# Retention followed by a gated feed-forward block: the row transposes of chunks 2 to 5 are issued by ScalarE instead of SyncE

## The chip, the cores and the metric

The kernel runs on one core of a Trainium2 chip. A core has five engines with an instruction queue each: TensorE (PE, matrix products), VectorE (DVE), ScalarE (ACT, activation functions and copies), GpSimd (POOL) and SyncE (SP, which here only issues DMAs). Every engine executes its own queue in order, and the queues meet only at semaphores. The metric is the device time of one execution in microseconds, lower is better.

## The reference

Two stages are joined. The first is a recurrence over 768 positions for 4 batches and 8 heads of 64 elements, with a decay per head:

```python
gamma = 1.0 - 2.0 ** (-5.0 - np.arange(H))
for t in range(S):
    state = gamma * state + einsum('bhd,bhe->bhde', k[:, :, t], v[:, :, t])
    y[:, :, t] = (1/sqrt(D)) * einsum('bhd,bhde->bhe', q[:, :, t], state)
```

Its 3072 rows of 512 (heads side by side) go through a feed-forward block:

```python
rms = sqrt(mean(x * x, axis=-1) + 1e-6)
xn = x / rms * rms_g
g = xn @ w_gate                      # 512 x 1536
out = (g * sigmoid(g) * (xn @ w_val)) @ w_out
```

Inputs and output are float32.

## The kernel before

The 768 positions are cut into 6 chunks of 128 positions. A piece of work belongs to a chunk c (0 to 5) and a batch b (0 to 3). Inside a chunk the recurrence is a masked product of q and k times v; between chunks a state per batch is carried. Matrix operands are bfloat16, sums are float32 in PSUM, which is used as eight banks.

The order of all work is written out by hand in the string ORDER (lines 17 to 100). Each word is one step: a letter for the function, then its arguments, after "@" the engine (D, A, P, S for DVE, ACT, POOL, SP) and after "/" the PSUM banks. Each engine executes its own steps in the order of the string; semaphores between engines, and between DMA queues, follow from the data and from buffer reuse. The steps that matter here, for one c and b:

- Lq, Lk, Lv load float32 rows (line 314, for these chunks on SP); Cq, Ck and V convert or scale them (V on ACT is eight calls, one a head, line 356). tq and tk transpose q and k by DMA on SP (line 387).
- A multiplies kT and qT into two banks for each batch it names (A.3.2/0546: batches 2 and 3 of chunk 3, banks 0 and 5, 4 and 6; line 403). M0 and M1 mask the result on DVE (line 426). Y multiplies it by v and adds the state's part (lines 441 and 445).
- S is ACT's sum of squares of y (xsq, line 458, or 455 where y lies in two banks). R makes 1/rms on POOL (lines 468, 470). N writes the normalised rows xn, 128 x 512, on DVE (line 482, or 479).
- The feed-forward block needs xn transposed, as xnT. In chunks 0 and 1 PE transposes it (X, line 495) and XE copies it out of PSUM. In chunks 2 to 5 there is no X: XE is a DMA transpose of xn into xnT, issued by SP (line 501).
- g and v multiply xnT by the two weights (line 549), 128 columns a step for all 512 rows of a chunk, so the first of them needs the XE of all four batches. s is Silu on ACT (line 559), which empties the bank of g; h multiplies by v's bank into hT on DVE (line 567).
- d multiplies hT by the output weights (line 574), o copies the result to o_sb on ACT or DVE (line 146, a helper), st stores it (line 587, SP). B and U carry the state (lines 541 and 534).

So the XE steps stand in SP's queue between loads, stores and the transposes of q and k. In the order string the 16 XE words of chunks 2 to 5 are XE.2.0, XE.2.1, XE.2.3, XE.2.2; XE.3.1 and, further down, XE.3.0, XE.3.2, XE.3.3; XE.4.0, XE.4.1, XE.4.3, XE.4.2; XE.5.0, XE.5.3, XE.5.2, XE.5.1.

xn has a ring of 4 buffers and xnT one of 2. DMA completions of SP are counted on eight semaphores in turn, so each DMA also waits until the one eight before it has landed.

Of the kernel before, what the change touches and what calls it, by code (L numbers as in the profile page):

```python
# [49 lines left out]
s.1.4.5.0.4 K.1.3/4 v.1.4.5.0.4/0 S.2.0 U.1.3@D v.1.5.6.0.4/1 Cq.3.1@P h.1.9.10.0.4 R.2.0 h.1.4.5.0.4 A.2.2/5264  # L50
h.1.5.6.0.4 N.2.0 Y.2.1/7 Lk.3.1@S M0.2.3 M0.2.2 V.2.3@P B.1.3 S.2.1 d.1.1.0.10/1 K.2.0/3 tq.3.0 Ck.3.1@A
d.1.1.10.12 M1.2.3 R.2.1 M1.2.2 tk.3.0 Lv.2.2@S Y.2.3/6 S.2.3 V.2.2@P d.1.0.0.10/0 K.2.1/2 Y.2.2/5 tq.3.1
Lk.3.2@S S.2.2 N.2.1 R.2.3 d.1.2.0.12/7 R.2.2 U.2.1@D o.1.1@A XE.2.0@S Lk.3.3@S tk.3.1 K.2.3/4 N.2.3 U.2.0@D
N.2.2 Lq.3.3@S XE.2.1@S d.1.3.0.12/3 U.2.3@D A.3.0/2641 M1.3.1 d.1.0.10.12 XE.2.3@S XE.2.2@S M0.3.1 st.0.3@S
M0.3.0 st.0.2@S st.0.0@S B.2.1 Lv.3.1@S g.2.5.6.0.4/5 Lv.3.0@S o.1.3@A g.2.0.1.0.4/1 v.2.8.9.0.4/4 s.2.5.6.0.4
v.2.5.6.0.4/2 s.2.0.1.0.4 M1.3.0 Lq.3.2@S Lq.4.1@S Ck.3.3@D g.2.10.11.0.4/6 g.2.1.2.0.4/1 h.2.5.6.0.4 o.1.0@A
v.2.10.11.0.4/0 g.2.8.9.0.4/2 B.2.0 Cq.3.3@P s.2.10.11.0.4 Lk.4.0@S s.2.8.9.0.4 o.1.2@A g.2.6.7.0.4/5
# [1 line left out]
g.2.11.12.0.4/3 V.3.1@A Cq.4.1@P s.2.6.7.0.4 Lv.3.2@S h.2.10.11.0.4 s.2.3.4.0.4 tk.3.3 Lq.4.0@S h.2.8.9.0.4  # L59
Lv.3.3@S K.3.1/2 s.2.1.2.0.4 h.2.3.4.0.4 tk.3.2 g.2.4.5.0.4/5 B.2.3 h.2.6.7.0.4 U.3.1@D V.3.2@D tq.3.2 Lq.5.0@S  # L60
st.1.0@S v.2.11.12.0.4/4 K.2.2/7 U.2.2@D s.2.11.12.0.4 Y.3.1/6 tq.4.1 st.1.2@S S.3.1 h.2.11.12.0.4 v.2.1.2.0.4/1
h.2.1.2.0.4 R.3.1 g.2.7.8.0.4/2 st.1.3@S v.2.7.8.0.4/4 Ck.4.1@P s.2.7.8.0.4 N.3.1 XE.3.1@S g.2.2.3.0.4/3
h.2.7.8.0.4 Ck.4.0@D s.2.4.5.0.4 st.1.1@S A.3.2/0546 M1.3.2 s.2.2.3.0.4 v.2.2.3.0.4/7 g.2.9.10.0.4/3 V.3.0@D
M0.3.2 V.3.3@A s.2.9.10.0.4 v.2.4.5.0.4/5 M1.3.3 h.2.2.3.0.4 Lk.5.2@S Y.3.0/2 Lv.4.0@S M0.3.3 v.2.9.10.0.4/6
Y.3.3/3 Lv.4.1@S B.2.2 K.3.3/7 S.3.0 h.2.4.5.0.4 S.3.3 R.3.0 K.3.0/5 h.2.9.10.0.4 Y.3.2/0 Lv.4.2@S Cq.4.0@P
d.2.2.0.12/1 R.3.3 K.3.2/4 N.3.0 S.3.2 N.3.3 d.2.1.0.10/2 d.2.1.10.12 XE.3.0@S Lq.5.2@S R.3.2 N.3.2 Ck.5.2@D
XE.3.2@S d.2.3.0.12/3 U.3.3@D XE.3.3@S U.3.2@D Lk.4.2@S o.2.2@D Lq.4.2@S Lv.5.3@S U.3.0@D d.2.0.0.10/4 tk.4.0
g.3.6.7.0.4/5 tk.4.1 o.2.3@A o.2.1@D g.3.0.1.0.4/0 v.3.6.7.0.4/7 s.3.6.7.0.4 tq.4.0 v.3.0.1.0.4/1 s.3.0.1.0.4
g.3.10.11.0.4/6 V.4.2@D B.3.1 Lv.4.3@S Lk.4.3@S Cq.5.0@P g.3.5.6.0.4/5 s.3.10.11.0.4 h.3.0.1.0.4 g.3.9.10.0.4/3
d.2.0.10.12 v.3.5.6.0.4/0 h.3.6.7.0.4 Lq.4.3@S s.3.5.6.0.4 v.3.9.10.0.4/1 v.3.10.11.0.4/2 h.3.5.6.0.4  # L70
# [6 lines left out]
M1.4.3 v.3.7.8.0.4/4 tq.5.2 M0.4.2 st.2.3@S M0.4.3 S.4.0 s.3.11.12.0.4 Y.4.1/0 h.3.7.8.0.4 M1.4.2 Cq.5.3@P R.4.0  # L77
v.3.11.12.0.4/7 h.3.11.12.0.4 K.4.1/4 Lv.5.1@S Y.4.2.2 S.4.1 Y.4.3.2 S.4.2 V.5.1@P d.3.1.0.10/6 tk.5.3 tk.5.2
N.4.0 R.4.1 tk.5.1 st.2.0@S d.3.1.10.12 S.4.3 tq.5.3 N.4.1 R.4.3 o.3.1@A R.4.2 d.3.0.0.10/1 B.4.3 N.4.3 Lq.5.1@S
XE.4.0@S XE.4.1@S N.4.2 U.4.1@D d.3.0.10.12 A.5.2/0457 Lk.5.0@S V.5.2@A Cq.5.1@P XE.4.3@S M0.5.2 XE.4.2@S  # L80
d.3.3.0.12/3 st.2.1@S o.3.0@D d.3.2.0.12/1 M1.5.2 Ck.5.0@A o.3.2@A o.3.3@D B.4.0 M0.5.3 B.4.1 v.4.11.12.0.4/5
tk.5.0 g.4.11.12.0.4/3 M1.5.3 g.4.0.1.0.4/2 s.4.0.1.0.4 s.4.11.12.0.4 h.4.11.12.0.4 g.4.2.3.0.4/7 s.4.2.3.0.4
v.4.0.1.0.4/6 g.4.8.9.0.4/4 g.4.7.8.0.4/3 tq.5.0 h.4.0.1.0.4 st.3.2@S tq.5.1 V.5.0@A A.5.0/6127 s.4.7.8.0.4
s.4.8.9.0.4 v.4.2.3.0.4/5 M1.5.1 st.3.1@S h.4.2.3.0.4 g.4.3.4.0.4/7 Y.5.3/3 S.5.3 M0.5.0 B.4.2 M1.5.0
v.4.8.9.0.4/5 Y.5.2/0 s.4.3.4.0.4 h.4.8.9.0.4 R.5.3 Y.5.0/4 M0.5.1 S.5.2 v.4.7.8.0.4/1 S.5.0 v.4.3.4.0.4/7 R.5.0
R.5.2 v.4.1.2.0.4/5 h.4.7.8.0.4 N.5.0 g.4.1.2.0.4/1 s.4.1.2.0.4 Y.5.1/4 g.4.6.7.0.4/6 S.5.1 st.3.0@S XE.5.0@S
N.5.3 g.4.4.5.0.4/2 h.4.3.4.0.4 h.4.1.2.0.4 s.4.6.7.0.4 v.4.6.7.0.4/1 g.4.9.10.0.4/3 XE.5.3@S v.4.9.10.0.4/5
R.5.1 s.4.4.5.0.4 N.5.2 v.4.4.5.0.4/2 XE.5.2@S N.5.1 XE.5.1@S g.4.10.11.0.4/6 h.4.6.7.0.4 v.4.5.6.0.4/1
s.4.10.11.0.4 v.5.6.7.0.4/7 h.4.4.5.0.4 s.4.9.10.0.4 g.5.1.2.0.4/6 h.4.9.10.0.4 g.4.5.6.0.4/2 g.5.6.7.0.4/4
v.4.10.11.0.4/5 s.5.6.7.0.4 h.5.6.7.0.4 g.5.3.4.0.4/4 h.4.10.11.0.4 g.5.2.3.0.4/0 s.4.5.6.0.4 s.5.3.4.0.4  # L90
h.4.5.6.0.4 v.5.3.4.0.4/7 h.5.3.4.0.4 v.5.9.10.0.4/3 s.5.1.2.0.4 d.4.0.0.10/6 d.4.1.0.10/5 v.5.1.2.0.4/2
# [12 lines left out]
def kernel(  # L104
# [14 lines left out]
    B, H, S, D = q.shape  # L119
# [21 lines left out]
    DVE, ACT, POOL, SP = nc.vector, nc.scalar, nc.gpsimd, nc.sync  # L141
# [3 lines left out]
    def copy(e, out, in_):  # L145
        (e.copy if e is ACT else e.tensor_copy)(out, in_)  # L146
# [10 lines left out]
    for h in range(H):  # L157
# [20 lines left out]
        out=darg, in0=pos_f[:, :, None].to_broadcast([128, NCH, H]),  # L178
# [24 lines left out]
    t = {(c, b): {} for c in range(NCH) for b in range(B)}  # L203
# [281 lines left out]
    def rows_of(c):  # L485
        if c not in xnT:
            xnT[c] = ring([128, KS, GT], BF16, "xnT", 2)
        return xnT[c]
# [6 lines left out]
            nc.tensor.transpose(u["xP"][:, s, :], u["xn"][:, s * 128:(s + 1) * 128], ident)  # L495

    @op
    def XE(e, bk, c, b):
        x = rows_of(c)[:, :, b * C:(b + 1) * C]
        if e is SP:  # L500
            SP.dma_start_transpose(out=x, in_=t[c, b]["xn"])
        else:
            copy(e, x, t[c, b]["xP"])

# [95 lines left out]
    for w in ORDER.split():  # L600
        w, _, bk = w.partition("/")
# [33 lines left out]
```

## Time and profile before

| | us |
|---|---|
| runs shown | 233.80, 235.77, 233.58 (median 233.8) |
| span of the profiled execution | 233.6 |
| PE busy in it | 227.6 |
| DVE busy | 130.4 |
| ACT busy | 96.1 |
| POOL busy | 89.7 |
| DMA issue to landing of an xnT transpose, median | 2.8 |

The span runs from the first to the last instruction of one profiled execution; no time is given for that execution beside its span, and the median of the runs is 0.2 us above it. Busy times are of work on the engine: instructions that only issue a DMA, wait or branch are not counted, so SP has no busy time. In a timeline row the first number is the start, the second the length, both in us, and the bracket at the end says how long the engine sat idle before and what ended it. SPq and POOLq are the issuing queues of SP and POOL.

### The profile page before, as it was taken

The numbers are of one execution on the slowest core, as the hardware profiler recorded it, in microseconds if no ns is written. First come the engines' busy times: TensorE is split into PE (matmuls) and PEld (weight loads), VectorE is DVE, ScalarE is ACT, GpSimd is POOL, SyncE is SP. The second block draws the span as 40 slices with busy tenths as digits, with TensorE's granted clock in tenths as the row PEclk, the third lists the DMA queues.
The fourth block names the chain that finished last, engine by engine and source line by source line (L and its number), as shares of the span: only waits on it lengthen the run. The fifth ranks groups of instructions, "written<-read, shape, count | busy, mean of one in ns | idle before, by whom it ended". The sixth has DMA issues, their size and how long they took to land.

```text
span 233.6 us, 4637 instructions
## 1 busy us (share of the span) xinstructions
PE 227.6 (97%) x1771; PEld 120.8 (52%) x1771; DVE 130.4 (56%) x241; ACT 96.1 (41%) x231; POOL 89.7 (38%) x163
## 2 busy tenths in 40 slices
PE   8799999999999999999999999999999999999994
PEld 2458855645545655445554444554455444444444
DVE  6479639753662965628975239866367532323320
ACT  7658433514337231464731346553265332232202
POOL 8958998550544555030273741247003100000000
PEclk9979999999999999999999999999999999999999
DMA  7999999999798888999988899968511400020222
GB/s 126 147 180 123 127 179 184 205 145 215 133 206 214 171 194 140 262 218 221 235 173 146 179 221 206 198 149 142 148 61 27 112 0 0 3 90 9 83 89 93
DMA packets 105353, 33.61 MB, mean 144 GB/s; under 512 B 94449, under 2 KB 102385, under 8 KB 105330
## 3 DMA queue, kind: packets, MB, share of 16 engines
q1 hardware_dynamic: 81858, 25.70, 50.2%
q0 software_dynamic: 23472, 7.60, 30.1%
q8 instruction: 14, 0.23, 0.4%
q14 instruction: 9, 0.07, 0.1%
HBM read 28.31 MB, written 6.29 MB: 148 GB/s over the span
## 4 chain that ended last, share of the span: by engine, by line
PE 89%; DMA 4%; POOL 2%; ACT 2%; DVE 1%; issue 0%; SPq 0%; POOLq 0%; DVEq 0%; ACTq 0%
PE v_ps L549 27%; PE g_ps L549 27%; PE o_ps L574 21%; PE a_ps L403 3%; DMA kb<-in_k_dram 3%; PE y_ps L441 2%; PE kv_ps L526 2%; PE y_ps L445 2%; DMA out_dram<-o_sb 1%; PE o_ps L596 1%; PE hot_ps L240 1%; PE t_ps L366 1%; PE t_ps L371 1%; PE xt_ps L495 1%; ACT xsq L455 1%; ACT xsq L458 1%
## 5 line engine op out<-in xcount | busy, mean ns | idle before, releaser
L567 DVE TENSOR_TENSOR hT<-sg,v_ps 128x512 bf16<-128x512 bf16 (+2 forms) x76 | 48.7, 656 | 47.8 <-PE v_ps L549 34.8
L549 PE MATMUL v_ps<-xnT,wv_b 128*128 128x512 bf16 (+2 forms) x344 | 71.2, 345 | 0.1
L559 ACT ACTIVATE sg<-g_ps 128x512 bf16<-128x512 f32 (+2 forms) x76 | 42.1, 575 | 70.6 <-PE g_ps L549 68.1
L549 PE MATMUL g_ps<-xnT,wg_b 128*128 128x512 bf16 (+2 forms) x344 | 70.0, 344 | 0.0
L574 PE MATMUL o_ps<-wo_b,hT 128*128 128x512 bf16 x276 | 63.5, 379 | 0.0
L549 PEld LDWEIGHTS <-wg_b 128*128 128x128 bf16 x344 | 30.4, 98 | 29.3
L549 PEld LDWEIGHTS <-wv_b 128*128 128x128 bf16 x344 | 30.2, 98 | 28.9 <-DVE am L426 0.6
L574 PEld LDWEIGHTS <-hT 128*128 128x128 bf16 x276 | 26.3, 98 | 29.1
L468 POOL TENSOR_SCALAR ms<-ssq 128x1 f32<-128x1 f32 x24 | 4.6, 190 | 59.1 <-ACT xsq L458 58.4
L426 DVE TENSOR_TENSOR am<-a_ps,causal 128x512 bf16<-128x512 f32 x32 | 20.6, 685 | 7.8 <-PE a_ps L403 7.5
L339 POOL TENSOR_TENSOR qb<-qf,ydec 128x512 bf16<-128x512 f32 x13 | 14.0, 1074 | 25.2 <-DMA qf<-in_q_dram 24.9
L146 ACT COPY o_sb<-o_ps 128x512 f32<-128x512 f32 (+1 forms) x16 | 8.8, 552 | 29.7 <-PE o_ps L574 23.1
L458 ACT ACTIVATE xsq<-y_ps 128x512 f32<-128x512 f32 x22 | 13.2, 599 | 18.9 <-PE y_ps L445 13.7
L482 DVE SCALAR_TENSOR_TENSOR xn<-y_ps,rstd,g_bc 128x512 bf16<-128x512 f32 x22 | 16.3, 748 | 4.3 <-POOL rstd L470 3.0
L146 DVE COPY o_sb<-o_ps 128x512 f32<-128x512 f32 (+1 forms) x10 | 6.4, 648 | 18.1 <-PE o_ps L574 12.2
L541 POOL CAST st_b<-st_f 64x256 bf16<-64x256 f32 x40 | 15.9, 398 | 1.3
L470 POOL TENSOR_TENSOR rstd<-ms,mhalf 128x1 f32<-128x1 f32 x24 | 13.3, 552 | 2.0
L534 DVE TENSOR_TENSOR st_f<-st_f,kv_ps 128x512 f32<-128x512 f32 x16 | 10.8, 684 | 5.2 <-PE kv_ps L526 4.6
L356 ACT ACTIVATE vp<-vf,vdec 128x64 bf16<-128x64 f32 x48 | 12.2, 343 | 0.0
L426 DVE TENSOR_TENSOR am<-a_ps,mask 128x512 bf16<-128x512 f32 x16 | 10.4, 686 | 2.5 <-PE a_ps L403 2.3
L240 PE MATMUL hot_ps<-one 128*128 128x512 bf16 x20 | 8.5, 547 | 1.1 <-DVE one L153 1.1
L441 PEld LDWEIGHTS <-am 128*128 128x128 bf16 x176 | 7.8, 99 | 3.1 <-issue 0.3
(99 smaller groups left out, 174.8 us busy)
## 6 DMA issues: line engine op xcount, KB each, us to landing
out_dram<-o_sb SPq DMA_DIRECT2D x23, 256.0 KB, 2.4
kf<-in_k_dram SPq DMA_DIRECT2D x18, 256.0 KB, 3.8
qf<-in_q_dram SPq DMA_DIRECT2D x16, 256.0 KB, 3.9
vf<-in_v_dram SPq DMA_DIRECT2D x16, 256.0 KB, 3.9
wo_b<-in_moe_w_out_dram POOLq DMA_DIRECT2D x3, 512.0 KB, 12.2
qb<-in_q_dram POOLq DMA_DIRECT2D x8, 128.0 KB, 6.6
vp<-in_v_dram POOLq DMA_DIRECT2D x8, 128.0 KB, 6.5
kb<-in_k_dram POOLq DMA_DIRECT2D x6, 128.0 KB, 5.9
```

The lines of the kernel that those rows point to most:

```text
L146: (e.copy if e is ACT else e.tensor_copy)(out, in_)
L339: e.tensor_tensor(out=u["qb"], in0=u["qf"], in1=ydec[:, c, :, None].to_broadcast([128, H, D]), op=ALU.mult)
L426: DVE.tensor_tensor(out=u["am"][:, i], in0=u["a"][i], in1=m, op=ALU.mult)
L441: nc.tensor.matmul(y[:, h, :], u["am"][:, h % 2, h // 2, :], u["vp"][:, h, :], start=h == 0, stop=c == 0 and h == H - 1, skip_group_check= ...
L458: ACT.activation(xsq, flat(u["y"]), AF.Square, accum_out=u["ssq"])
L470: POOL.tensor_tensor(out=u["rstd"], in0=ms, in1=mhalf, op=ALU.pow)
L482: DVE.scalar_tensor_tensor(out=u["xn"], in0=flat(u["y"]), scalar=u["rstd"], in1=g_bc, op0=ALU.mult, op1=ALU.mult)
L541: POOL.tensor_copy(st_b[b][r, :, i * 64:i * 64 + 64], st_f[b][r, :, i * 64:i * 64 + 64])
L549: nc.tensor.matmul(p[:, (n - n0) * m:(n - n0 + 1) * m], W[w][0][:, s, n * 128:(n + 1) * 128], xnT[c][:, s, b0 * C:b1 * C], start=s == 0, s ...
L559: ACT.activation(sg[:, :cols], done["wg", c, n0, b0][:, :cols], AF.Silu)
L567: DVE.tensor_tensor(out=hT[c][:, n0:n1, b0 * C:b1 * C], in0=sg, in1=p, op=ALU.mult)
L574: nc.tensor.matmul(o_ps[c, b], hT[c][:, n, b * C:(b + 1) * C], wo_b[:, n, :], start=n == 0, stop=n == NFF - 1)
```

## The change

The 16 XE words of chunks 2 to 5 get a fourth argument, 1, and the engine A instead of S. The function takes this argument (near) and issues the same DMA transpose on the engine that it is given. All words keep their places in the string. The first of the changed lines of ORDER, and the function:

```diff
-Lk.3.2@S S.2.2 N.2.1 R.2.3 d.1.2.0.12/7 R.2.2 U.2.1@D o.1.1@A XE.2.0@S Lk.3.3@S tk.3.1 K.2.3/4 N.2.3 U.2.0@D
-N.2.2 Lq.3.3@S XE.2.1@S d.1.3.0.12/3 U.2.3@D A.3.0/2641 M1.3.1 d.1.0.10.12 XE.2.3@S XE.2.2@S M0.3.1 st.0.3@S
+Lk.3.2@S S.2.2 N.2.1 R.2.3 d.1.2.0.12/7 R.2.2 U.2.1@D o.1.1@A XE.2.0.1@A Lk.3.3@S tk.3.1 K.2.3/4 N.2.3 U.2.0@D
+N.2.2 Lq.3.3@S XE.2.1.1@A d.1.3.0.12/3 U.2.3@D A.3.0/2641 M1.3.1 d.1.0.10.12 XE.2.3.1@A XE.2.2.1@A M0.3.1 st.0.3@S
...
     @op
-    def XE(e, bk, c, b):
+    def XE(e, bk, c, b, near=0):
         x = rows_of(c)[:, :, b * C:(b + 1) * C]
-        if e is SP:
-            SP.dma_start_transpose(out=x, in_=t[c, b]["xn"])
+        if e is SP or near:
+            e.dma_start_transpose(out=x, in_=t[c, b]["xn"])
         else:
             copy(e, x, t[c, b]["xP"])
```

As built, the order of instructions on PE, DVE and POOL is the same. On ACT the transposes stand at these places: the four of chunk 2 between the copies o.1.1 and o.1.3; XE.3.1 between two Silu calls (the second is s.2.4.5), the other three of chunk 3 behind three xsq and ahead of the copy o.2.3; XE.4.0 and XE.4.1 behind the copy o.3.1, then the eight calls of V.5.2, then XE.4.3 and XE.4.2 ahead of Ck.5.0; XE.5.0 behind the last xsq of chunk 5, then a Silu, XE.5.3, a Silu, XE.5.2 and XE.5.1. In SP's queue they are gone, and what stood behind them moves up. The built program also has waits between the two issuers of transposes: the first ACT transpose of a group waits for the landing of SP's earlier transposes, and SP's next transpose waits for the landing of ACT's.

More of the change, by code (lines that the diff above doesn't have):

```diff
@@ L61 @@
 st.1.0@S v.2.11.12.0.4/4 K.2.2/7 U.2.2@D s.2.11.12.0.4 Y.3.1/6 tq.4.1 st.1.2@S S.3.1 h.2.11.12.0.4 v.2.1.2.0.4/1
-h.2.1.2.0.4 R.3.1 g.2.7.8.0.4/2 st.1.3@S v.2.7.8.0.4/4 Ck.4.1@P s.2.7.8.0.4 N.3.1 XE.3.1@S g.2.2.3.0.4/3
+h.2.1.2.0.4 R.3.1 g.2.7.8.0.4/2 st.1.3@S v.2.7.8.0.4/4 Ck.4.1@P s.2.7.8.0.4 N.3.1 XE.3.1.1@A g.2.2.3.0.4/3
 h.2.7.8.0.4 Ck.4.0@D s.2.4.5.0.4 st.1.1@S A.3.2/0546 M1.3.2 s.2.2.3.0.4 v.2.2.3.0.4/7 g.2.9.10.0.4/3 V.3.0@D
@@ L65 @@
 Y.3.3/3 Lv.4.1@S B.2.2 K.3.3/7 S.3.0 h.2.4.5.0.4 S.3.3 R.3.0 K.3.0/5 h.2.9.10.0.4 Y.3.2/0 Lv.4.2@S Cq.4.0@P
-d.2.2.0.12/1 R.3.3 K.3.2/4 N.3.0 S.3.2 N.3.3 d.2.1.0.10/2 d.2.1.10.12 XE.3.0@S Lq.5.2@S R.3.2 N.3.2 Ck.5.2@D
-XE.3.2@S d.2.3.0.12/3 U.3.3@D XE.3.3@S U.3.2@D Lk.4.2@S o.2.2@D Lq.4.2@S Lv.5.3@S U.3.0@D d.2.0.0.10/4 tk.4.0
+d.2.2.0.12/1 R.3.3 K.3.2/4 N.3.0 S.3.2 N.3.3 d.2.1.0.10/2 d.2.1.10.12 XE.3.0.1@A Lq.5.2@S R.3.2 N.3.2 Ck.5.2@D
+XE.3.2.1@A d.2.3.0.12/3 U.3.3@D XE.3.3.1@A U.3.2@D Lk.4.2@S o.2.2@D Lq.4.2@S Lv.5.3@S U.3.0@D d.2.0.0.10/4 tk.4.0
 g.3.6.7.0.4/5 tk.4.1 o.2.3@A o.2.1@D g.3.0.1.0.4/0 v.3.6.7.0.4/7 s.3.6.7.0.4 tq.4.0 v.3.0.1.0.4/1 s.3.0.1.0.4
@@ L79 @@
 N.4.0 R.4.1 tk.5.1 st.2.0@S d.3.1.10.12 S.4.3 tq.5.3 N.4.1 R.4.3 o.3.1@A R.4.2 d.3.0.0.10/1 B.4.3 N.4.3 Lq.5.1@S
-XE.4.0@S XE.4.1@S N.4.2 U.4.1@D d.3.0.10.12 A.5.2/0457 Lk.5.0@S V.5.2@A Cq.5.1@P XE.4.3@S M0.5.2 XE.4.2@S
+XE.4.0.1@A XE.4.1.1@A N.4.2 U.4.1@D d.3.0.10.12 A.5.2/0457 Lk.5.0@S V.5.2@A Cq.5.1@P XE.4.3.1@A M0.5.2 XE.4.2.1@A
 d.3.3.0.12/3 st.2.1@S o.3.0@D d.3.2.0.12/1 M1.5.2 Ck.5.0@A o.3.2@A o.3.3@D B.4.0 M0.5.3 B.4.1 v.4.11.12.0.4/5
@@ L85 @@
 v.4.8.9.0.4/5 Y.5.2/0 s.4.3.4.0.4 h.4.8.9.0.4 R.5.3 Y.5.0/4 M0.5.1 S.5.2 v.4.7.8.0.4/1 S.5.0 v.4.3.4.0.4/7 R.5.0
-R.5.2 v.4.1.2.0.4/5 h.4.7.8.0.4 N.5.0 g.4.1.2.0.4/1 s.4.1.2.0.4 Y.5.1/4 g.4.6.7.0.4/6 S.5.1 st.3.0@S XE.5.0@S
-N.5.3 g.4.4.5.0.4/2 h.4.3.4.0.4 h.4.1.2.0.4 s.4.6.7.0.4 v.4.6.7.0.4/1 g.4.9.10.0.4/3 XE.5.3@S v.4.9.10.0.4/5
-R.5.1 s.4.4.5.0.4 N.5.2 v.4.4.5.0.4/2 XE.5.2@S N.5.1 XE.5.1@S g.4.10.11.0.4/6 h.4.6.7.0.4 v.4.5.6.0.4/1
+R.5.2 v.4.1.2.0.4/5 h.4.7.8.0.4 N.5.0 g.4.1.2.0.4/1 s.4.1.2.0.4 Y.5.1/4 g.4.6.7.0.4/6 S.5.1 st.3.0@S XE.5.0.1@A
+N.5.3 g.4.4.5.0.4/2 h.4.3.4.0.4 h.4.1.2.0.4 s.4.6.7.0.4 v.4.6.7.0.4/1 g.4.9.10.0.4/3 XE.5.3.1@A v.4.9.10.0.4/5
+R.5.1 s.4.4.5.0.4 N.5.2 v.4.4.5.0.4/2 XE.5.2.1@A N.5.1 XE.5.1.1@A g.4.10.11.0.4/6 h.4.6.7.0.4 v.4.5.6.0.4/1
 s.4.10.11.0.4 v.5.6.7.0.4/7 h.4.4.5.0.4 s.4.9.10.0.4 g.5.1.2.0.4/6 h.4.9.10.0.4 g.4.5.6.0.4/2 g.5.6.7.0.4/4
```

## The prediction, made before the changed kernel ran

> **What bounds the kernel now.** I read the page's totals first, then busy time by stretches.
>
> ```profile
> span 233.6 us, 4637 instructions
> ...
> PE 227.6 (97%) x1771; PEld 120.8 (52%) x1771; DVE 130.4 (56%) x241; ACT 96.1 (41%) x231; POOL 89.7 (38%) x163
> ...
> PE 89%; DMA 4%; POOL 2%; ACT 2%; DVE 1%; issue 0%; SPq 0%; POOLq 0%; DVEq 0%; ACTq 0%
> ```
>
> TensorE (PE) is busy for 97% of the span. The chain that ended last is 89% PE, and SP's queue (SPq) is 0% of it. In the stretches in which the changed transposes run (columns: length, then busy time of PE, PEld, DVE, ACT, POOL; granted clock, DMA share, GB/s):
>
> ```profile
> 85.00:110.00 25.00, 25.00 (x172) 12.55 (x169) 13.68 (x23) 10.29 (x25) 5.88 (x13) 1.00 1.01 206
> ...
> 157.00:170.00 13.00, 12.76 (x72) 5.72 (x71) 6.58 (x12) 5.07 (x15) 4.95 (x12) 1.00 0.69 154
> 170.00:190.00 20.00, 20.00 (x147) 10.12 (x146) 11.52 (x18) 8.88 (x24) 2.96 (x8) 1.00 0.19 46
> ```
>
> PE has no idle time there but 13.00 - 12.76 = 0.24 us. So there is nothing to gain beyond about 0.2 us, and whatever makes PE wait is added to the span in full. PE executes in order: one late operand stops everything behind it.
>
> **The change, part by part.** Removed from SP: sixteen transposes. Added to ScalarE (ACT), at the same places of the written order: the same sixteen.
>
> ```profile
> L501 SPq DMA_TRANSPOSE xnT<-xn x16: 1188/1216/1842, 83.3 to 183.2; - x16
> ...
> DMA to landing us min/median/max: 2.4/2.8/4.8
> ```
>
> SP holds its queue 1.22 us for each (median), so SP gets 16 x 1.22 = 19.5 us back. PE does not wait for SP, so this is worth 0. It moves SP's stores and loads earlier, about 5 us at chunk 2, into a stretch where the DMA share is 1.01 already; I keep that for a rival.
>
> ACT pays 19.5 us of issuing. In sum that is harmless, 96.1 + 19.5 us of 233.6. But ACT also runs in order, and an issue waits until the row block xn is written and then blocks the copies and Silu calls behind it. No row of before shows a transpose issued by ACT. Its issue time I bound by 0.33 us, the shortest store of the row under the rivals, and 1.84 us above; I take 1.22, the same operation on the neighbouring queue. Whether an issue can run beside the ACT operation just before it I bound both ways ("beside" and "after"). Now the five places.
>
> Chunk 2, four transposes behind the copy o.1.1:
>
> ```profile
> 89.03 0.58 ACT L146 COPY o_sb<-o_ps 128x512 f32<-128x512 f32 x1
> ...
> 90.08 0.75 DVE L482 SCALAR_TENSOR_TENSOR xn<-y_ps,rstd,g_bc 128x512 bf16<-128x512 f32 x1 [0.23 <-POOL rstd L470]
> ...
> 94.44 0.31 PEld L549 LDWEIGHTS <-wg_b 128*128 128x128 bf16 x2
> ```
>
> SP had issued the first at 83.3, and the last when its xn was ready. On ACT all four stand behind the copy, which ends at 89.03 + 0.58 = 89.61; the last xn is ready at 90.83. After the copy: the fourth starts at 89.61 + 3 x 1.22 = 93.27 and lands 2.8 later at 96.07, while PE loads weights for it at 94.44: **1.6 us** of stall. Beside the copy, from 89.1, and with 2.4 to landing: 89.1 + 3.66 + 2.4 = 95.16, **0.7 us**. Next in ACT's queue is the copy at 94.4, which is not held.
>
> Chunk 3, first transpose, XE.3.1, between two Silu calls:
>
> ```profile
> 111.30 1.09 ACT L559 ACTIVATE sg<-g_ps 128x512 bf16<-128x512 f32 x2 [0.98 <-PE g_ps L549]
> ...
> 111.34 0.75 DVE L482 SCALAR_TENSOR_TENSOR xn<-y_ps,rstd,g_bc 128x512 bf16<-128x512 f32 x1 [0.22 <-POOL rstd L470]
> ...
> 112.92 0.62 PE L403 MATMUL a_ps<-qT,kT 64*128 64x128 bf16 x16
> ```
>
> ACT ran both calls back to back, the second done at 112.39. Now it must wait for xn at 111.34 + 0.75 = 112.09, issue until 113.31, and end the second call (0.60 long, as in the chunk 5 rows below) at 113.91. That call, s.2.4.5, empties PSUM bank 5, which PE's A.3.2 (banks 0, 5, 4, 6) overwrites at 112.92: **1.0 us**, under either bound. Queued behind it are two Silu calls, the eight vp calls between them and three xsq; PE, 1.0 us later itself, finds them in time.
>
> Chunk 3, the other three:
>
> ```profile
> 121.32 0.75 DVE L482 SCALAR_TENSOR_TENSOR xn<-y_ps,rstd,g_bc 128x512 bf16<-128x512 f32 x1 [0.16 <-POOL rstd L470]
> ...
> 126.95 0.59 ACT L146 COPY o_sb<-o_ps 128x512 f32<-128x512 f32 x1 [7.22 <-PE o_ps L574]
> ...
> 128.69 0.74 PEld L549 LDWEIGHTS <-wg_b 128*128 128x128 bf16 x4
> ```
>
> ACT idles 7.22 us there. The last two go at 122.07 and 123.29 and land by 126.1, before 128.69: **0**.
>
> Chunk 4, two transposes, the eight vp calls, two more:
>
> ```profile
> 156.73 0.59 ACT L146 COPY o_sb<-o_ps 128x512 f32<-128x512 f32 x1 [0.98 <-PE o_ps L574]
> 157.21 2.03 ACT L356 ACTIVATE vp<-vf,vdec 128x64 bf16<-128x64 f32 x8
> ...
> 165.58 0.55 PEld L549 LDWEIGHTS <-wv_b 128*128 128x128 bf16 x4 [0.61 <-DVE am L426]
> ...
> 171.73 0.45 PEld L403 LDWEIGHTS <-kT 64*128 64x128 bf16 x16 [0.42 <-issue]
> ```
>
> After the copy: 157.32 + 2.44 = 159.76, vp until 161.79, the fourth starts at 163.01 and lands at 165.8: **0.2 us** past 165.58. Beside it the fourth starts near 162.3 and lands before PE asks; the earlier stores may then free DVE's copies and give back the 0.24 idle: **-0.2**. SP's next q and k transposes wait for this landing: three and a store, 165.8 + 3 x 1.22 + 0.6 + 1.2 (the landing less its issue) = 171.3, just before 171.73.
>
> Chunk 5, four transposes alternating with Silu calls:
>
> ```profile
> 180.94 0.20 ACT L458 ACTIVATION_READ_ACCUMULATOR xsq<-y_ps 128x1 f32 x1
> 181.23 0.60 ACT L559 ACTIVATE sg<-g_ps 128x512 bf16<-128x512 f32 x1
> ...
> 186.86 0.53 PEld L549 LDWEIGHTS <-wv_b 128*128 128x128 bf16 x3
> ```
>
> After: from 181.14, issue to 182.36, Silu to 182.96, issue to 184.18, Silu to 184.78, issue to 186.00, and the fourth lands at 186.00 + 2.4 (the DMA share is 0.19 here) = 188.4, against 186.86: **1.5 us**. Beside, both Silu calls cost no time in the issue chain but their dispatch: the fourth starts near 184.9, lands at 187.3: **0.4**.
>
> Sum, after: 1.6 + 1.0 + 0 + 0.2 + 1.5 = 4.3; beside: 0.7 + 1.0 + 0 - 0.2 + 0.4 = 1.9. No row decides between them, so I take the middle, 3.1. On the profiled execution's 233.6 that is 236.7; the median of the runs is 0.2 above that span, so **236.9**, own range 233.8 + 1.9 to 233.8 + 4.3, 235.7 to 238.1.
>
> **The rivals.**
>
> *Covered (not slower).* ACT may hand a transpose to its queue quickly instead of being held 1.22 us.
>
> ```profile
> L587 SPq DMA_DIRECT2D out_dram<-o_sb x26: 332/402/1622, 71.5 to 230.8; - x26
> ```
>
> At 0.33 us each, chunk 2 ends with its last xn (90.83 + 2.8 = 93.6, no stall), chunk 3's Silu ends at 112.09 + 0.33 + 0.60 = 113.02 (0.1), and chunk 5's last starts near 183.1 and lands at 185.5 (0). With the -0.2 of chunk 4 this gives 233.7. It decides below (94.44 - 2.4 - 89.61) / 3 = 0.8 us per issue at chunk 2 and 112.92 - 112.09 - 0.60 = 0.23 us at chunk 3. Against it: the smallest of sixteen is 1188 ns.
>
> The Trainium skill, page "DMA: Bandwidth & Descriptors", section "Issuing engines are not separate DMA queues", says that issuing from several engines only saves sequencer time, usually small beside the DMA. By that rule the cost would be about this rival's. The trace disagrees as to small: 1.2 of 2.8 us is the issue.
>
> *Crowded landings.* SP's stores and loads, freed by 5 us, now fill the DMA engines beside ACT's transposes. With 4.8 us to landing, chunk 2 costs 93.27 + 4.8 - 94.44 = 3.6 and chunk 4 163.01 + 4.8 - 165.58 = 2.2; with 1.0 and 1.5 the sum is 8.3: 242.1. For it: DMA share 1.01 at chunk 2. Issues of 1.84 us instead, at landings of 2.8 and 2.4, would cost 3.5 + 1.6 + 2.1 + 3.4 = 10.6, 244.4, the far end. Against: on a queue of their own the transposes no longer stand behind those loads, and 4.8 and 1.84 are each the largest of sixteen.
>
> *Held by SP (the queue is not its own).* The built program makes the first ACT transpose of each group wait until all earlier q and k transposes of SP have landed, and SP's next one until ACT's have. Mostly these are long done; the close one is at chunk 3:
>
> ```profile
> 109.24 1.74 SPq L387 DMA_TRANSPOSE qT<-qb  x1
> ```
>
> With 2.8 it lands at 112.0, before xn at 112.09; with 4.8 at 114.0, 1.9 us later than I count. Added to the forecast: 238.8. Against it: SP runs earlier in the new kernel.
>
> The Trainium skill, same page, section "Silent corruption: two transposing streams in flight at once", demands this wait for transposes from two engines, since both results can be corrupted otherwise. It speaks against the change, and no run here shows two such streams yet.
>
> **How the numbers follow.** Forecast 0.58, covered 0.18, crowded 0.16, held 0.08. A measurement here tells about 1%, 2.3 us, so slower begins at 236.1: a sixth of the forecast's cases (0.10) lies below, 0.48 above. Slower 0.48 + 0.16 + 0.08 = 0.72; same 0.10 + 0.18, less 0.01 left for faster, which no case reaches, 0.27. The range 234.3 to 241.0 leaves out half of covered (0.10) and the upper half of crowded (0.08), with its far end.
>
> **What would show it.** Right: transposes of about 1.2 us among ACT's instructions; the first g matmul of chunk 2 released by an xnT landing, 0.7 to 1.6 us late; A.3.2 released by the Silu of line 559; the first chunk 5 matmul released by xnT; chunk 4 unchanged; PE idle between 85 and 190 up from 0.2 to about 3 us. Wrong: ACT's issue rows well under 0.8 us with PE as busy as before, landings above 4 us at chunks 2 and 4, or PE waiting for q and k transposes of SP.

## The result and the profile after

The changed kernel takes 241.7 us (median of 240.92, 241.39, 242.02 and 243.63); the kernel before took 233.96 beside it. The ratio is 1.0338, 95% interval 1.0280 to 1.0395: 7.7 us slower, where 3.1 were forecast and the range ended at 241.0.

The profiled execution of the changed kernel took 241.39 us at a span of 239.7, so a time here is its span plus 1.7. The profiled execution of the kernel before, with its span of 233.6, was therefore some 1.5 to 2 us slower than its median. The busy times of the first 20 us show where (the columns are as in the prediction; first the kernel before, then the changed one):

```profile
0.00:20.00 20.00, 17.39 (x239) 9.73 (x240) 13.34 (x50) 13.95 (x32) 15.36 (x32) 0.91 1.33 154
```
```profile
0.00:20.00 20.00, 18.80 (x282) 11.55 (x283) 15.89 (x55) 15.95 (x38) 17.71 (x37) 1.00 1.36 161
```

The granted clock was 0.91 there, against 1.00, and PE did 239 matmuls instead of 282. This lies ahead of the change, so I compare the two executions from A.3.0 on, the last step of PE ahead of chunk 2's feed-forward block. The page of the changed kernel:

```profile
PE 227.6 (95%) x1747; PEld 120.7 (50%) x1771; DVE 130.6 (54%) x241; ACT 95.9 (40%) x231; POOL 89.6 (37%) x163
...
PEclk9999999999999999599999999999999999999999
...
PE 84%; DMA 6%; POOL 3%; issue 2%; ACT 2%; DVE 1%; ACTq 1%; DVEq 0%; POOLq 0%
```

PE is busy for just as long, though each figure has slow matmuls in it (the first 20 us of before, one slice of after). DMA has 6% of the chain that ended last instead of 4%. One slice of the 40, from 96 to 102 us, has a granted clock of 0.5. From A.3.0 on, PE's waits name two new ones of more than 0.3 us, each a single stop (columns: in all, times, longest):

```profile
PE g_ps L549 <- DMA xnT<-xn: 3.8, 1, 3.8
PE a_ps L403 <- ACT sg L559: 1.3, 1, 1.3
```

PE's rows at five places give the account. Of the kernel before:

```profile
93.66 0.62 PE L403 MATMUL a_ps<-qT,kT 64*128 64x128 bf16 x16
...
94.66 1.89 PE L549 MATMUL g_ps<-xnT,wg_b 128*128 128x512 bf16 x8
...
159.22 0.96 PE L403 MATMUL a_ps<-qT,kT 64*128 64x128 bf16 x16
...
165.58 1.04 PE L549 MATMUL v_ps<-xnT,wv_b 128*128 128x512 bf16 x4
...
187.94 2.75 PE L549 MATMUL g_ps<-xnT,wg_b 128*128 128x512 bf16 x12
```

The same of after:

```profile
91.82 0.62 PE L403 MATMUL a_ps<-qT,kT 64*128 64x128 bf16 x16
...
96.82 2.29 PE L549 MATMUL g_ps<-xnT,wg_b 128*128 128x512 bf16 x5 [3.84 <-DMA xnT<-xn]
...
117.64 0.23 PE L403 MATMUL a_ps<-qT,kT 64*128 64x128 bf16 x1
...
165.43 0.96 PE L403 MATMUL a_ps<-qT,kT 64*128 64x128 bf16 x16
...
171.51 1.03 PE L549 MATMUL v_ps<-xnT,wv_b 128*128 128x512 bf16 x4
...
193.98 2.75 PE L549 MATMUL g_ps<-xnT,wg_b 128*128 128x512 bf16 x12
```

| stretch, from one row's start to the next | before | after | added |
|---|---|---|---|
| A.3.0 to the first g of chunk 2 (stop) | 1.00 | 5.00 | 4.0 |
| first g of chunk 2 to A.3.2 | 18.26 | 20.82 | 2.6 |
| A.3.2 to the A step ahead of chunk 4's feed-forward block | 46.30 | 47.79 | 1.5 |
| that A step to the first v of chunk 4 | 6.36 | 6.08 | -0.3 |
| that v to a run of twelve g in chunk 5 | 22.36 | 22.47 | 0.1 |

(A.3.2 of before is the row at 112.92 in the prediction; in the changed kernel its first matmul is at 117.64.) The sum is 7.9 us against 7.7 between the medians. Behind the last row nothing is added: the spans differ by 6.1, and these last rows by 6.04. (That is less than 7.9 by the 1.84 us by which the profiled kernel before came later to A.3.0.)

The second term is the slow slice. The stretches of the changed kernel:

```profile
92.60:96.80 4.20, 0.38 (x2) 0.01 (x1) 2.70 (x5) 0.50 (x1) 0.59 (x1) 0.81 1.34 222
96.80:102.00 5.20, 4.96 (x12) 1.85 (x14) 0.00 (x0) 1.67 (x3) 1.19 (x3) 0.50 0.80 179
102.00:106.00 4.00, 4.00 (x20) 1.80 (x19) 1.02 (x2) 0.60 (x1) 0.00 (x0) 1.00 0.61 134
```

PE stopped for 4 us, and behind the stop it ran 5.2 us at a granted clock of 0.50: 12 matmuls there, against 20 in the 4.0 us that follow. Half of 5.2 is the 2.6 lost.

ACT's issues at chunk 2, and the last transpose in the chain (start, length, what):

```profile
86.89 1.50 ACTq L501 DMA_TRANSPOSE xnT<-xn  x1
...
87.19 0.58 ACT L146 COPY o_sb<-o_ps 128x512 f32<-128x512 f32 x1
88.43 3.98 ACTq L501 DMA_TRANSPOSE xnT<-xn  x3
```
```profile
91.18 5.50 DMA xnT<-xn
```

ACT starts the first issue before the copy that stands ahead of it in the order has begun, and each issue takes 1.2 to 1.5 us. But the last transpose, issued at 91.18, lands 5.5 us later, where 2.4 to 2.8 were expected. SP's queue at that time:

```profile
83.97 1.60 SPq L587 DMA_DIRECT2D out_dram<-o_sb  x3
85.61 1.69 SPq L314 DMA_DIRECT2D vf<-in_v_dram  x2
88.32 2.04 SPq L314 DMA_DIRECT2D qf<-in_q_dram  x2
90.63 3.24 SPq L314 DMA_DIRECT2D kf<-in_k_dram  x2
```

The same queue in the kernel before:

```profile
87.19 4.85 SPq L501 DMA_TRANSPOSE xnT<-xn  x3
92.09 1.54 SPq L587 DMA_DIRECT2D out_dram<-o_sb  x3
```

There SP issued its three stores at 92.09, behind the four transposes, 1.6 us ahead of A.3.0; now the stores go out 7.9 us ahead of A.3.0, and they and six loads are issued around the transposes.

### The profile page after: what moved, and what is told of

Read it like the earlier page. It is cut to its first block, busy times and chain, and to the rows that moved or that the text cites. A ratio compares the mean times of both kernels' runs of the same rounds, so it can differ in the third digit from the quotient of the medians.

```text
span 239.7 us, 4610 instructions
## 1 busy us (share of the span) xinstructions
PE 227.6 (95%) x1747; PEld 120.7 (50%) x1771; DVE 130.6 (54%) x241; ACT 95.9 (40%) x231; POOL 89.6 (37%) x163
## 4 chain that ended last, share of the span: by engine, by line
PE 84%; DMA 6%; POOL 3%; issue 2%; ACT 2%; DVE 1%; ACTq 1%; DVEq 0%; POOLq 0%
PE v_ps L549 25%; PE g_ps L549 24%; PE o_ps L574 21%; DMA wg_b<-in_moe_w_gate_dram 3%; PE a_ps L403 2%; PE hot_ps L240 2%; DMA xnT<-xn 2%; PE y_ps L441 2%; PE y_ps L445 2%; PE kv_ps L526 2%; POOL rstd L470 1%; PE o_ps L596 1%; PE t_ps L366 1%; PE t_ps L371 1%; POOL wv_b L323 1%
## 5 line engine op out<-in xcount | busy, mean ns | idle before, releaser
L574 PE MATMUL o_ps<-wo_b,hT 128*128 128x512 bf16 x266 | 62.5, 379 | 0.5
L403 PE MATMUL a_ps<-qT,kT 64*128 64x128 bf16 x192 | 8.4, 217 | 1.4 <-ACT sg L559 1.3
```

The source lines that it names most:

```text
L403: nc.tensor.matmul(u["a"][i][:, hp, :], u["kT"][r, hp, :], u["qT"][r, hp, :], start=True, stop=True)
L574: nc.tensor.matmul(o_ps[c, b], hT[c][:, n, b * C:(b + 1) * C], wo_b[:, n, :], start=n == 0, stop=n == NFF - 1)
```

## The experiments

After the result my theory was: two separate costs at chunk 2, late landings because SP's freed traffic goes first, and a clock that halves behind the stop; and a third at chunk 3, where ACT waits in front of a Silu. The main rival was that the issues themselves, on ACT, cost it: then it would not matter what SP does, nor which chunk is taken out, but how many there are.

### Chunk 2 back on SP, and chunk 2 alone

The first kernel gives the four XE words of chunk 2 back to SP; the second leaves only these four on ACT (of each other chunk the first word is shown).

```diff
-... o.1.1@A XE.2.0.1@A ... XE.2.1.1@A ... XE.2.3.1@A XE.2.2.1@A
+... o.1.1@A XE.2.0@S ... XE.2.1@S ... XE.2.3@S XE.2.2@S
```
```diff
-... XE.3.1.1@A ... XE.4.0.1@A ... XE.5.0.1@A
+... XE.3.1@S ... XE.4.0@S ... XE.5.0@S
```

> The changed kernel, but chunk 2's four transposes are back on SP; chunks 3 to 5 stay on ScalarE. Theory (nearly all of the loss is chunk 2: a PE gap of 4.0 us, then matmuls at half the granted clock for another 3.4 us; chunk 3 adds 1.3): 234.0 + 1.3 = about 235.3, no PE gap before g of chunk 2, no slow matmuls. Rival (the loss is spread over the groups, about a quarter each of 7.7): 241.7 - 1.9 = 239.8.

> Only chunk 2's four transposes on ScalarE, chunks 3 to 5 on SP. Theory (chunk 2 is nearly all): 241.7 - 1.3 = about 240.4, with the 4 us gap and the half clock. Rival (spread evenly): 234.0 + 1.9 = 235.9.

Without chunk 2: 236.78 us, ratio 1.0128 (1.0065 to 1.0191). Chunk 2 alone: 241.46, ratio 1.0313 (1.0261 to 1.0366). So chunk 2 alone, a quarter of the issues, is as slow as the whole change, which the count of issues does not explain. (The two losses do not add up to the whole: with chunk 2 alone PE's idle time there is 5.38 us instead of 3.84, and the stop at A.3.2 is absent.) Without chunk 2 the median is above the 235.3 expected, but the single times lie in two groups: 235.35 and 235.69, as expected, and 237.86 and 238.09. The profile is of the 235.35:

```profile
113.13 0.60 PE L403 MATMUL a_ps<-qT,kT 64*128 64x128 bf16 x15 [1.90 <-ACT sg L559]
```

The stop at A.3.2 is 1.9 us instead of 1.3. What sets the upper group apart is taken up by a later experiment.

### SP's stores held back

The first store of the group (and with it all that stands behind it on SP) waits for the landing of XE.2.3, the third of chunk 2's four on ACT (after, in the code, adds that wait). All sixteen transposes stay on ACT.

```diff
+        if (c, b) == (0, 3):
+            after(i_, ("XE", 2, 3))
```

> The changed kernel, but SP's first store behind chunk 2's q and k transposes waits until the third ScalarE transpose of chunk 2 has landed; the loads behind it wait with it. So SP's traffic starts about when it did before the change. Theory (the landings of 5.4 to 6.5 us come from SP's earlier stores and loads): landings of 2.4 to 3.2 us, PE gap under 1 us, no half clock: 234.0 + 0.6 + 1.3 = about 235.9. Rival (a transpose issued by ScalarE lands late here whatever SP does): landings stay above 5 us, 241.7.

238.31 us, ratio 1.0205 (1.0157 to 1.0253). The transposes of chunk 2 in this kernel, against the changed one (the line's own view, same window, this experiment first):

```profile
L501 ACTq DMA_TRANSPOSE xnT<-xn x4: 1231/1284/1302, 87.4 to 91.3; - x4
...
DMA to landing us min/median/max: 2.5/2.5/2.7
```
```profile
L501 ACTq DMA_TRANSPOSE xnT<-xn x4: 1231/1281/1501, 86.9 to 91.2; - x4
...
DMA to landing us min/median/max: 5.5/5.7/6.3
```

Same engine, issue times within 0.5 us, and the landing falls from 5.7 to 2.5 us. The stop at chunk 2 shrinks to an idle time of 0.71 us and the clock stays at 1.00. So the late landing is shown to come from SP's traffic. The total missed its 235.9 by 2.4 us. Of this, 1.5 is the stop at chunk 3, which grew from 1.29 to 2.79 us; the rest has no row of its own.

```profile
115.44 0.60 PE L403 MATMUL a_ps<-qT,kT 64*128 64x128 bf16 x15 [2.79 <-ACT sg L559]
```
```profile
110.26 1.22 SPq L387 DMA_TRANSPOSE qT<-qb  x1
```
```profile
DMA to landing us min/median/max: 3.1/3.1/3.1
```
```profile
113.52 1.23 ACTq L501 DMA_TRANSPOSE xnT<-xn  x1
114.79 1.08 ACT L559 ACTIVATE sg<-g_ps 128x512 bf16<-128x512 f32 x2 [3.40 <-issue]
```

The four fences are PE, SP, the landing of that transpose of q, and ACT. xn was written at 110.84 + 0.75 = 111.59, but ACT issued at 113.52, behind the landing of SP's transpose at 110.26 + 3.1 = 113.36. That is the "held by SP" rival of the prediction, with its 1.9 us. In the changed kernel the same wait is 0.4 us (xn at 116.81, SP's transpose issued at 112.21 lands 4.9 later, at 117.11, ACT issues at 117.25). The Silu starts 0.04 us after the issue ends, and its bracket names only the issue: it waited for nothing else that the profile shows.

### Only the loads held back

As above, but the stores go early and the loads from the first vf on wait.

```diff
+        if (n, c, b) == ("v", 3, 1):
+            after(i, ("XE", 2, 3))
```

> The changed kernel, but only the loads behind SP's three stores wait until the third ScalarE transpose of chunk 2 has landed; the stores go early. Theory (DMAs land about in the order in which both queues issued them, so only what was issued shortly before a transpose delays it): the first transposes land late, 3.5 to 5 us, behind the stores, the last in under 3.5; gap of 1 to 2 us, no half clock, span 236 to 237. Rival (the stores alone are the block): gap of 3 us or more and half clock, span 239 or more.

One time, 237.9 us, beside 234.7 before. The landings of chunk 2, least to most, and PE:

```profile
DMA to landing us min/median/max: 2.5/3.1/4.8
```
```profile
114.01 0.60 PE L405 MATMUL a_ps<-qT,kT 64*128 64x128 bf16 x15 [1.76 <-ACT sg L561]
...
116.23 1.90 PE L551 MATMUL g_ps<-xnT,wg_b 128*128 128x512 bf16 x4
```

With the stores alone in front the first transpose, issued at 87.1, takes the 4.8 us, and the last, issued at 91.2, lands in 2.5. PE waits for the last one, and in the changed kernel that one took 5.5, so the part of the delay that PE felt comes from the loads. PE's rows name lines two higher, those of this kernel. The span of 236.2 us lies in the range that I expected, but not by its terms: PE's stop at chunk 2 is down to 0.58 us, and I expected no half clock. There is one, behind the stop at chunk 3: the four g matmuls at 116.23 take 1.90 us, where four took 1.03 at full clock. That stop is 1.76 us.

### The stop at chunk 2 filled with matmuls

The theory here was that the half clock follows from the length of the stop. Matmuls of a constant, whose result nothing uses, are put ahead of the first g of chunk 2: eighteen, then eight.

```diff
-... B.2.1 Lv.3.1@S g.2.5.6.0.4/5
+... B.2.1 Lv.3.1@S H.18/5 g.2.5.6.0.4/5
```

> The changed kernel with 18 matmuls of 128x512 on constants put on PE ahead of the first g of chunk 2, so that PE works through its 4 us wait. They compute nothing that is used. Theory (the granted clock halves because PE stood still): clock stays at 1, 241.7 - 3.4 = about 238.3, the wait itself stays. Rival (those matmuls are slow for another reason, such as the DMA traffic on their operands): still 0.43 us apart, 241.7.

> As with the 18 matmuls on constants ahead of g of chunk 2, but 8, which fill about 1.8 us of the wait; 2.5 to 3.5 us of standing still are left. Theory (a stop of 2.8 us left the clock alone elsewhere, one of 4.0 us halved it, so the limit lies between): no half clock if the stop stays under about 3 us, 241.7 - 3 = 238.7. Rival (any stop of about 2 us ahead of this g halves it): 241.7 as before.

Eighteen: 239.92 us, ratio 1.0262 (1.0228 to 1.0295). Eight: 241.26, ratio 1.0282 (1.0227 to 1.0336), beside a kernel before of 234.7 on that chip. PE with eighteen, then with eight:

```profile
92.50 4.05 PE L240 MATMUL hot_ps<-one 128*128 128x512 bf16 x18
97.61 1.89 PE L549 MATMUL g_ps<-xnT,wg_b 128*128 128x512 bf16 x8 [1.07 <-DMA xnT<-xn]
```
```profile
98.40 2.29 PE L549 MATMUL g_ps<-xnT,wg_b 128*128 128x512 bf16 x7 [2.97 <-DMA xnT<-xn]
100.49 3.21 PE L549 MATMUL v_ps<-xnT,wv_b 128*128 128x512 bf16 x8
```

With eighteen, g waits for the same late landing, but runs at full clock (eight matmuls in 1.89 us); the kernel is 1.8 us faster than the changed one and not 3.4, as the last landing was later here: g starts 6.1 us behind A.3.0 (at 91.50), against 5.0, and 1.1 of the 2.6 us of the half clock are lost again. So the half clock is a cost of its own, and at this stop it comes of PE doing nothing. With eight, an idle time of 2.97 us is left and the clock is halved again (eight matmuls in 3.21 us): the miss of 241.26 against 238.7 falls on the length that I had guessed to be safe.

### The late Silu at chunk 3

XE.3.1 is moved down, from between the two Silu calls to just ahead of XE.3.0. Once with chunk 2 on SP, once with all sixteen on ACT and SP's stores held.

```diff
-... s.2.7.8.0.4 N.3.1 XE.3.1.1@A g.2.2.3.0.4/3
+... s.2.7.8.0.4 N.3.1 g.2.2.3.0.4/3
...
-... d.2.1.0.10/2 d.2.1.10.12 XE.3.0.1@A
+... d.2.1.0.10/2 d.2.1.10.12 XE.3.1.1@A XE.3.0.1@A
```

> Chunks 3 to 5 on ScalarE, chunk 2 on SP, and the first transpose of chunk 3, XE.3.1, moved down ScalarE's queue from between two Silu calls to ahead of XE.3.0. Theory (the 2.9 us that chunks 3 to 5 cost are XE.3.1 holding the Silu that frees PSUM bank 5): no gap at A.3.2, back to about 234.0. Rival (the issuing on ScalarE in chunks 4 and 5 costs it): stays near 236.8.

> All sixteen on ScalarE, SP's stores of chunk 2 held as before, and XE.3.1 moved as well. Theory (two causes, each taken away; what stays is the 1.1 us gap ahead of g of chunk 2): 234.0 + 1.1 = about 235.0. Rival (a cost of ScalarE's issuing that neither edit touches): 236 or more.

With chunk 2 on SP: 234.31 us, ratio 0.9998 (0.9977 to 1.0019): the whole remaining loss of the first experiment is gone. With all sixteen on ACT and SP held: 235.41, ratio 1.0053 (1.0028 to 1.0077). PE in the second of them:

```profile
93.87 1.89 PE L549 MATMUL g_ps<-xnT,wg_b 128*128 128x512 bf16 x7 [0.71 <-DMA xnT<-xn]
...
129.34 1.89 PE L549 MATMUL g_ps<-xnT,wg_b 128*128 128x512 bf16 x7 [1.06 <-DMA xnT<-xn]
```

A.3.2 no longer stops: these two are the only waits for a transpose, and none for the Silu is left. What is left is 0.71 us at chunk 2 and 1.06 at chunk 3, whose last transposes now come late. With the two collisions out of the way, all sixteen transposes on ACT cost 1.3 us (235.41 against 234.12).

### Chunks 4 and 5 alone, and chunk 4 alone

The first kernel of this pair gives chunks 2 and 3 back to SP, the second chunk 5 too.

```diff
-... XE.2.0.1@A ... XE.3.1.1@A ... XE.5.0.1@A
+... XE.2.0@S ... XE.3.1@S ... XE.5.0.1@A
```
```diff
-... XE.2.0.1@A ... XE.3.1.1@A ... XE.5.0.1@A
+... XE.2.0@S ... XE.3.1@S ... XE.5.0@S
```

> Only the eight transposes of chunks 4 and 5 on ScalarE. Theory (chunk 4 gains about 0.5 us, because DVE's copies no longer wait for a store that stood behind SP's transposes; chunk 5 loses about 0.5): about 233.9, no change. Rival (issuing on ScalarE costs its 1.2 us beside the Silu calls): chunk 5 alone 1.5, 235.4.

> Only the four transposes of chunk 4 on ScalarE. Theory: 0.5 us gained, about 233.4. Rival (the gain at chunk 4 is given back later, in chunk 5): 233.9.

Chunks 4 and 5: 233.34 us, ratio 0.9969 (0.9945 to 0.9994). Chunk 4 alone: 233.23, ratio 0.9976 (0.9955 to 0.9997). Both lie 0.2 to 0.3% below the kernel before, with intervals that end just below 1: at most a small gain. In the changed kernel the trace shows 0.3 us gained ahead of the first v of chunk 4, which is 0.1% of the time; the rest of the 0.3% has no row of its own. Chunk 5 on ACT adds nothing that the times show.

### The first experiment's kernel twice more

It is the kernel with chunk 2 back on SP again.

> The kernel of the first experiment again (chunk 2's transposes back on SP), for a second profile. Its times before lay in two groups, about 235.5 and about 238.0 us, and the profile there, at full clock throughout, belongs to the lower. If the upper group are executions in which the clock is halved after the stop of PE at chunk 3 (2.1 us in the profile), a profile of 238 us shows matmuls 0.427 us apart behind that stop, and one of 235.5 us does not. If the groups have another cause, a profile of 238 us has full clock and the stretch is longer elsewhere.

> The same kernel, for a third profile; the same expectation. If the length of the stop alone decides on the clock, the three profiles agree: stops of 2.1 us, full clock, some 233.6 us of span.

235.52 and 234.84 us, with 233.67 before beside them: both lie with the lower group. Their stops at A.3.2 read 1.70 and 1.60 us, the clock behind them 1.00 in both:

```profile
113.16 0.60 PE L403 MATMUL a_ps<-qT,kT 64*128 64x128 bf16 x15 [1.70 <-ACT sg L559]
```

There is no profile of the upper group. What the runs do give is the mean granted clock of every execution: 1.0 for 235.35 and 235.69, 0.993 for 237.86 and 238.09. The upper group therefore lost some clock, and the mean does not tell where. The loads-held kernel has 0.993 with its half clock behind the stop at chunk 3. But the profile of the kernel before has 0.993 too, lost in its first 20 us, and so has that of chunk 4 alone: 235.25 us, about 2 us above most of its executions, with a clock of 0.91 in the first 20 us and no stop at chunk 3. A loss of clock at the start, which has nothing to do with the change, accounts for the upper group as well as a half clock at chunk 3 does; this stays open.

## Why the prediction was wrong, step by step

**What bounds the kernel: right, but not the whole.** PE is the limit, and what it waits for is added in full. At chunk 2 more than that was added, since the stop also slowed the work behind it.

**Chunk 2, the step that failed.** The term was 0.7 to 1.6 us; measured 4.0, and 2.6 more behind it, for which the sum had no term. Its first half held: issues of 1.2 to 1.5 us, the first beside the copy ("beside"), the last at 91.18. In the time of the kernel before, 1.84 us later from A.3.0's rows, this is 93.02, between the 92.76 that "beside" implies and the 93.27 of "after". The mis-sized part is the landing, taken as 2.4 and 2.8 us and measured at 5.5 to 6.3; with SP's stores and loads held back it is 2.5 to 2.7. The sentence that fell is the one against the crowded rival: that on a queue of their own the transposes no longer stand behind SP's loads. The views of the two lines in the changed kernel, for a load of q that SP issued at 88.3 and for the transposes that ACT issued at 86.9 and 88.4:

```profile
L314 SPq DMA_DIRECT2D qf<-in_q_dram x1: 1144/1144/1144, 88.3 to 88.3; - x1
...
DMA to landing us min/median/max: 6.3/6.3/6.3
```
```profile
L501 ACTq DMA_TRANSPOSE xnT<-xn x2: 1300/1400/1501, 86.9 to 88.4; - x2
...
DMA to landing us min/median/max: 5.7/6.0/6.3
```

The slower of the two transposes, the one issued at 88.4, lands 6.3 us later, and so does the load issued at 88.3: the transposes landed as if in one line with SP's traffic. Only the last one, issued at 91.2, lands a little ahead of a load of k issued 0.6 us before it (5.5 us beside 6.7). The Trainium skill, page "DMA: Bandwidth & Descriptors", section "Issuing engines are not separate DMA queues", says that DMAs of all issuers run on the same sixteen engines and interleave; I had used the section only for its other half, on what an issue costs. The trace agrees (6.3 beside 6.3 us; 2.5 when SP is held). The Trainium skill, same page, section "Queues, rings and completion order", has each DMA engine take turns between its queues packet by packet. These landings, nearly in the order of issue, do not tell how the turns were taken.

**The half clock: a term of 2.6 us put at nothing.** No row of before shows a PE stop in this stretch, so no price for what follows one could be read there; but a rival that prices a stop of 3.6 us should have asked. By the crowded rival's 8.3 the total would have been 242.1, close to the 241.7 measured, though by other terms: it had 2.2 at chunk 4 and 1.5 at chunk 5, and neither came.

**Chunk 3, XE.3.1: right in mechanism, a little small.** 1.0 forecast; the row reads 1.29, released by the Silu of line 559 as named, and 0.4 of it is SP's transpose of q holding ACT. That rival was right as a mechanism, with 0.4, 0.9 and 1.9 us in three kernels (in the first experiment SP's transpose was issued at 107.41 and landed 3.5 later, at 110.91, against an xn at 110.15 and ACT's issue at 111.07). I had played it down because SP runs earlier. It did, but little: the transpose of q was issued 4.6 us ahead of xn in the changed kernel, against 2.9 in the kernel before, and it landed after 4.9 us and not the 2.8 taken.

**The other three of chunk 3: 0, right.** PE's waits name no second stop by xnT. The last two transposes, issued at 128.3 and 129.6, took 3.2 to 3.7 us to land, more than the 2.8 taken; the slack ahead of the first g of chunk 3, at 135.12, covered it.

**Chunk 4: -0.2 to 0.2 forecast, -0.3 measured.** The idle 0.61 us at the weight load of before is gone. The vp calls and the issues do lie beside each other:

```profile
166.06 1.20 ACTq L501 DMA_TRANSPOSE xnT<-xn  x1
166.09 1.53 ACT L356 ACTIVATE vp<-vf,vdec 128x64 bf16<-128x64 f32 x6
```

Six calls, which stand ahead of that issue in the order, ran from 166.09 to 167.62, beside the issue from 166.06 to 167.26.

**Chunk 5: 0.4 beside, 1.5 after; measured 0.1.** "Beside" was the right bound. The weight load there sat idle for 0.43 us, about as forecast, but PE lost only 0.13 of it: its eight v took 2.02 us instead of 1.89, and its waits name no xnT. I had priced the lateness of the weight load as if it were PE's. The issue that follows a Silu in the order starts 0.03 us behind it and runs beside it:

```profile
187.82 0.60 ACT L559 ACTIVATE sg<-g_ps 128x512 bf16<-128x512 f32 x1 [0.77 <-PE g_ps L549]
187.85 1.25 ACTq L501 DMA_TRANSPOSE xnT<-xn  x1
```

**The base.** I put the profiled execution 0.2 us below the median; it was some 1.5 to 2 us slower than the median, by the clock of its first 20 us. Since the forecast was added to the median in effect, this did no harm to the number.

With every term at its measured size the sum is 4.0 + 2.6 + 1.5 - 0.3 + 0.1 = 7.9; with the two at chunk 2 as forecast it would have been about 2.5.

## What to carry to other kernels

When DMAs move to another engine's queue, price not only the issues that move but also the traffic that moves up on the queue they left: it goes out earlier, and here the transposes landed behind it, some 3 us later than with that traffic held back. A landing time read from a stretch with a different backlog is not a price; take it from rows where as much is in flight. When a forecast lets PE stop for some 2 us (1.76 is the shortest stop here with a half clock behind it), look for a half clock and price it apart.

## What was not expected of the hardware

- A DMA transpose of 1.2 us on ACT's queue is issued while ACT still works on what stands ahead of it in the order (the Silu at 187.82, the vp calls at 166.09). What stood behind it waited for its end: the Silu of chunk 3 started 0.04 us after it, at 118.50 in the changed kernel and at 114.79 with SP's stores held.
- The granted clock halves behind some stops of PE and not others, and the idle time alone does not tell which: halved behind 3.84 (changed kernel), 5.38 (chunk 2 alone), 2.97 (eight constant matmuls) and 1.76 us (loads held); full behind 2.79 (stores held), 1.90, 1.70 and 1.60 (first kernel, three profiles; the 2.1 of the expectations is the first of these from start to start).
- In three profiles the half clock lasted 3.4 us or twice that, taking the clock as either 1 or a half: in the changed kernel 0.81 over 4.20 us and 0.50 over the next 5.20 make 2 x 0.19 x 4.20 + 5.20 = 6.8 us, of which PE had work in 5.2. Chunk 2 alone gives 6.8 as well (0.90 over 5.30 and 0.61 over 7.40 us), the loads-held kernel 3.4 (0.57 over 4.00). In the changed kernel it began inside the stop; in the loads-held kernel the clock was 1.00 up to 114.00, where PE resumed, and it fell behind that.

The Trainium skill, page "TensorE: Matmul & The Clock Gate", section "What's actually happening", tells of an activity window of about 3.4 us that runs freely, so that the same stop may or may not fill one. That the length alone does not decide agrees with the rows, and so do half clocks of 3.4 and twice 3.4 us; that 1.76 us with fifteen short matmuls after it was enough in one kernel does not agree with a whole idle window. What decides stays open.
